# Strassen's scheme for the up products of a two-layer MLP behind linear attention: seven block products for eight, and the sums that go with it

## The chip, the cores and the metric

The kernel runs on one core of a Trainium2 chip. Times are device microseconds of one execution. Of the engines, PE multiplies matrices (PEld is its weight load), DVE works on vectors, ACT on pointwise functions and copies, POOL is GpSimd, SP issues the transfers.

## The reference

```python
def phi(x):
    proj = np.einsum('bhsd,df->bhsf', x, w_phi)
    proj = proj - np.max(np.abs(proj), axis=-1, keepdims=True)
    return np.concatenate([np.exp(proj), np.exp(-proj)], axis=-1)
...
x = attn_out.transpose(0, 2, 1, 3).reshape(2304, 512)   # linear attention, 4 x 576 tokens, 8 heads of 64
x = (sigmoid(x @ w_gate) * (x @ w_val)) @ w_out         # first layer, 512 -> 1536 -> 512
h = x @ w_in2                                           # second layer, 512 -> 2048
return np.maximum(0.01 * h, h) @ w_out2                 # 2048 -> 512
```

The weights arrive as float64 and are decoded from their bit pairs on the chip. Every product of the two layers is made of float32 operands split in two parts, hi + lo, each in the narrower fp32r type; a product is three matmuls, hi x hi, hi x lo and lo x hi (`mm3`, L50).

## The kernel before

Tokens lie on the free axis in blocks: four of 512 (one per batch) and one of 256 (the 64 last tokens of each batch, "the remainder"). The attention comes first (to about 275 us), with the first units of layer one between its pieces. Then layer one, six chunks of 256 hidden columns, and layer two, four chunks of 512 hidden columns, go through the five blocks each.

A unit is one chunk of hidden columns for one block. Its up products (`up2`, L513) run over four tiles of 128 hidden columns and four k tiles, into the PSUM banks `pg` and `pv` in turn. ACT scales the result by 0.01 (L522), DVE takes the maximum of both (L523), ACT rounds it to `gh` (L47) and DVE subtracts to give `gl` (L48). The down products (`down2`) give one 128-token piece after the other, `po`, accumulated over the chunk's tiles; DVE adds each to the sum of the chunks in SBUF (L542). The unit's down products come behind the first up tile of the next unit.

The next chunk's weights are decoded meanwhile: two masks (L77, L79), an exponent shift on ACT (L78), three DVE steps with two inputs (L80, L82, L83), a rounding on ACT (L84) and a subtraction for the low part (L86), each 128x512, for half a weight tile at a time. Steps of it are taken between the up tiles (`step`, DK).

The program's order on each engine is set by a scheduler from the order of the code. Engines hold to it.

```python
            nc.scalar.activation(out=th, in_=pg, func=ACTF.Copy, scale=0.01)
            nc.vector.tensor_tensor(out=th, in0=th, in1=pg, op=ALU.max)
            hidden(h, th, w)
```

Of the kernel before, what the change touches and what calls it, by code (L numbers as in the profile page):

```python
# [18 lines left out]
def linear_attention_moe(ctx, tc, q, k, v, w_phi, w_gate, w_val, w_out, w_in2, w_out2, out):  # L19
# [30 lines left out]
    def mm3(ps, lh, ll, rh, rl, first, last):  # L50
        nc.tensor.matmul(ps, lh, rh, start=first, stop=False)  # L51
        nc.tensor.matmul(ps, lh, rl, start=False, stop=False)  # L52
        nc.tensor.matmul(ps, ll, rh, start=False, stop=last)  # L53

    xh = [xp.tile([128, KD, w], F32R, name=f"xh{i}") for i, w in enumerate(bw)]
    xl = [xp.tile([128, KD, w], F32R, name=f"xl{i}") for i, w in enumerate(bw)]

# [1 line left out]
    CH1, CH2 = 2, 4  # L59
    NC1, NC2 = FF1 // CH1, FF2 // CH2  # L60
    NSLOT = 16
    slots = [0]
    pools = {}

    def slot():
        i = slots[0] % NSLOT
        slots[0] += 1
        pool = wpa if i < 6 else pools["wpb"]
        return pool.tile([128, 1024], F32R, tag=f"w{i}", name=f"w{i}")

    def decode(raw, hi, lo, expo):
        dp = pools["dec"]
        high, low = raw[:, :, 1], raw[:, :, 0].bitcast(U32)
        e = dp.tile([128, 512], I32, tag="e", name="e")
        m = dp.tile([128, 512], I32, tag="m", name="m")
        mf, ef = m.bitcast(F32), e.bitcast(F32)
        nc.vector.tensor_scalar(out=e, in0=high, scalar1=0x7FF00000, scalar2=0, op0=ALU.bitwise_and, op1=ALU.bitwise_or)  # L77
        nc.scalar.activation(out=e, in_=e, func=ACTF.Relu, scale=8.0, bias=ebias)  # L78
        nc.vector.tensor_scalar(out=m, in0=high, scalar1=0xFFFFF, scalar2=0x100000, op0=ALU.bitwise_and, op1=ALU.bitwise_or)  # L79
        nc.vector.scalar_tensor_tensor(out=mf, in0=low, scalar=2.0 ** -32, in1=m, op0=ALU.mult, op1=ALU.add)  # L80
        yield
        nc.vector.scalar_tensor_tensor(out=e, in0=high, scalar=-2 ** 31, in1=e, op0=ALU.bitwise_and, op1=ALU.bitwise_or)  # L82
        nc.vector.scalar_tensor_tensor(out=mf, in0=mf, scalar=2.0 ** expo, in1=ef, op0=ALU.mult, op1=ALU.mult)  # L83
        nc.scalar.copy(hi, mf)  # L84
        yield
        nc.vector.tensor_tensor(out=lo, in0=mf, in1=hi.bitcast(F32), op=ALU.subtract)  # L86
        yield

    def load_w(dst, src, r0, nr, c0, n, expo=-20):
        """Rows r0.. and columns c0.. of a weight matrix, rows on the partitions."""  # L90
        hi, lo = slot(), slot()
        dst.append([t.rearrange("p (k f) -> p k f", f=n) for t in (hi, lo)])
        kp = 512 // n
        raws = []
        for k0 in range(0, nr // 128, kp):
            raw = pools["dec"].tile([128, 512, 2], I32, tag="raw", name="raw", bufs=2)
            nc.sync.dma_start(
                out=raw.rearrange("p (k f) t -> p k (f t)", k=kp),
                in_=src[r0 + 128 * k0:r0 + 128 * (k0 + kp), 2 * c0:2 * (c0 + n)].rearrange("(k p) f -> p k f", p=128),
            )  # L100
            raws.append(raw)
        yield
        for i, raw in enumerate(raws):
            cs = slice(i * 512, i * 512 + 512)
            yield from decode(raw, hi[:, cs], lo[:, cs], expo)

    wts = {}

# [13 lines left out]
    def hidden(h, src, w):  # L122
        hi = pools["hp"].tile([128, 512], F32R, tag="gh", name="gh")[:, :w]
        lo = pools["hp"].tile([128, 512], F32R, tag="gl", name="gl")[:, :w]
        split(src, hi, lo)
        h.append((hi, lo))

    def up1(c, b, h):
        w = bw[b]
        for f in range(CH1):  # L130
            fs = slice(128 * f, 128 * f + 128)
            ps = []
            for i in range(2):
                wh, wl = wts[1, c][i]
                p = ps_m.tile([128, 512], F32, tag=("pg", "pv")[i], name=("pg", "pv")[i])[:, :w]
                ps.append(p)
                for kk in range(KD):
                    yield 0, kk
                    mm3(p, wh[:, kk, fs], wl[:, kk, fs], xh[b][:, kk], xl[b][:, kk], kk == 0, kk == KD - 1)
# [5 lines left out]
            yield 1, KD - 1  # L145

    acc = {}
    accd = {}

    def down1(c, b, h):  # L150
        (wh, wl) = wts[1, c][2]
        w = bw[b]
        for e in range(KD):
            es = slice(128 * e, 128 * e + 128)
            po = pools["po"].tile([128, 512], F32, tag="po", name="po")[:, :w]
            for f in range(CH1):
                if f:
                    yield 0
                mm3(po, wh[:, f, es], wl[:, f, es], h[f][0], h[f][1], f == 0, f == CH1 - 1)
            if c == 0 and b < B - 1:  # L160
                st = pools["tp"].tile([128, 512], F32, tag="st", name="st")
                nc.scalar.copy(st, po)
                nc.sync.dma_start(out=accd[b][:, e], in_=st)
            elif c == 0:
                nc.scalar.copy(acc[b][:, e], po)
            elif c < NC1 - 1:
                nc.vector.tensor_tensor(out=acc[b][:, e], in0=acc[b][:, e], in1=po, op=ALU.add)
            else:
# [12 lines left out]
    # Head pairs whose products with w_phi, or with the sums over k, are plain float32 ones: four passes,  # L181
    # without the work of splitting the operands, where the other engines have more to do than TensorE.
# [6 lines left out]
    # Products while the first loads are under way bring the tensor engine up to its full clock.  # L189
# [4 lines left out]
    # v of a head pair beside ones: [v_e | 1 | v_o]; the remainder's rows belong to one head each.  # L194
# [8 lines left out]
    # k_p^T [v | 1] of a pair: [kv_e | z_e | 0 | z_o | kv_o], so that 128 columns from 0 or 65 give a head.  # L203
# [38 lines left out]
    def parts(ps, n, tag, b, c):  # L242
        """The operand parts of a transposed tile: (float32,) or (hi, lo)."""
# [22 lines left out]
    def proj(x, c0, n, tag, bufs):  # L266
        """t = x @ w_phi - max|x @ w_phi| for n token tiles of a head pair."""
# [13 lines left out]
    def features(t, n, tag, bufs):  # L281
        """[exp(t), exp(-t)], tokens on the partitions."""
# [35 lines left out]
    def kv_main(p, s):  # L318
        """k_p^T [v | 1] for exp(t) or exp(-t): per head the sums of k_p v and of k_p."""
# [93 lines left out]
    pools["dec"] = p0.enter_context(tc.tile_pool(name="dec0", bufs=2))  # L413
    mid = ExitStack()
# [197 lines left out]
```

## Time and profile before

| | us |
|---|---|
| runs (3) | 1081.26, 1082.25, 1083.78; median 1082.25 |
| span of the profiled execution | 1081.0 |
| that execution's own time | one of the kernel's, not given apart; the median stands 1.25 over the span |
| PE busy | 1059.7 (98%) |
| DVE, ACT, POOL busy | 659.8 (61%), 433.9 (40%), 50.7 (5%) |
| first up product of layer two to the last down product | 680 to 1076 |

The span runs from the first to the last instruction. A matmul's duration overlaps with the next one's, so that the distance of two starts, not the duration, is what it costs; DVE's and ACT's operations overlap a little in the same way.

### The profile page before, as it was taken

The page shows a single profiled execution, that of the slowest core. Times are in us where ns is not written, and L with a number is a line of the kernel's source. Part 1 is how long each engine was busy: PE and PEld are TensorE (multiplying, and loading weights), DVE is VectorE, ACT ScalarE, POOL GpSimd, SP SyncE. Part 2 cuts the span into 40 slices and gives each one's busy share as a digit, 9 for nine tenths or more (in the row PEclk, how much of TensorE's full clock was granted, in tenths as well). Part 3 has the DMA queues.
Part 4 walks back from the last instruction along what each step waited for, and adds up shares of the span by engine and source line. Part 5 has one row for each costly group of instructions (what it writes and reads, how often), then busy time and mean ns, then how long its engine had stood idle before and what let it go on. Part 6 is the DMA issues. An engine that isn't in the chain of part 4 may idle for free.

```text
span 1081.0 us, 14504 instructions
## 1 busy us (share of the span) xinstructions
PE 1059.7 (98%) x5602; PEld 904.3 (84%) x5602; DVE 659.8 (61%) x1177; ACT 433.9 (40%) x925; POOL 50.7 (5%) x49
## 2 busy tenths in 40 slices
PE   8899999999999999999999999999999999999998
PEld 7788988889788888888888888888888888888887
DVE  5965777866489984493573774942494376333333
ACT  4665676766453431131231342533442243122121
POOL 0122121211200000000000000000000000000000
PEclk9999999999999999999999999999999999999999
DMA  6533243231363330030120210210130020000111
GB/s 156 142 79 76 64 111 75 69 87 43 93 233 115 117 97 20 1 118 1 40 78 1 75 43 1 79 39 1 39 117 2 1 78 1 1 1 20 59 39 59
DMA packets 85204, 66.69 MB, mean 62 GB/s; under 512 B 64912, under 2 KB 65040, under 8 KB 84752
## 3 DMA queue, kind: packets, MB, share of 16 engines
q1 hardware_dynamic: 85136, 65.77, 20.7%
q8 instruction: 44, 0.72, 0.3%
q14 instruction: 24, 0.20, 0.1%
HBM read 57.74 MB, written 7.94 MB: 61 GB/s over the span
## 4 chain that ended last, share of the span: by engine, by line
PE 72%; DVE 1%; issue 0%; DVEq 0%
PE po L51 10%; PE po L52 10%; PE po L53 10%; PE ph L52 6%; PE ph L51 6%; PE ph L53 6%; PE pv L51 4%; PE pv L53 4%; PE pv L52 4%; PE pg L51 4%; PE pg L52 4%; PE pg L53 4%; DVE th L143 0%; DVE e L82 0%; DVE m L80 0%
## 5 line engine op out<-in xcount | busy, mean ns | idle before, releaser
L47 ACT CAST gh<-th 128x512 fp32r<-128x512 f32 (+1 forms) x140 | 81.4, 581 | 144.3 <-DVE th L143 90.6
L48 DVE TENSOR_TENSOR gl<-th,gh 128x512 fp32r<-128x512 f32 (+1 forms) x140 | 89.1, 637 | 48.4 <-ACT gh L47 48.1
L52 PE MATMUL ph<-xl,w 128*128 128x512 f32 (+1 forms) x320 | 117.7, 368 | 0.0
L51 PE MATMUL ph<-xh,w 128*128 128x512 f32 (+1 forms) x320 | 117.7, 368 | 0.0
L53 PE MATMUL ph<-xh,w 128*128 128x512 f32 (+1 forms) x320 | 117.7, 368 | 0.0
L51 PE MATMUL po<-w,gh 128*128 128x512 f32 x288 | 112.1, 389 | 0.0
L52 PE MATMUL po<-w,gh 128*128 128x512 f32 x288 | 112.1, 389 | 0.0
L53 PE MATMUL po<-w,gl 128*128 128x512 f32 x288 | 112.0, 389 | 0.0
L522 ACT ACTIVATE th<-ph 128x512 f32<-128x512 f32 (+1 forms) x80 | 44.3, 554 | 162.8 <-PE ph L53 162.3
L523 DVE TENSOR_TENSOR th<-th,ph 128x512 f32<-128x512 f32 (+1 forms) x80 | 50.6, 632 | 75.8 <-ACT th L522 75.1
L51 PE MATMUL pv<-xh,w 128*128 128x512 f32 (+1 forms) x240 | 88.9, 370 | 1.2 <-DVE th L143 1.2
L51 PE MATMUL pg<-xh,w 128*128 128x512 f32 (+1 forms) x240 | 89.0, 371 | 0.6 <-ACT xh L47 0.6
L52 PE MATMUL pg<-xl,w 128*128 128x512 f32 (+1 forms) x240 | 89.2, 372 | 0.2 <-DVE xl L48 0.2
L53 PE MATMUL pg<-xh,w 128*128 128x512 f32 (+1 forms) x240 | 89.0, 371 | 0.0
L51 PE MATMUL po<-gh,w 128*128 128x512 f32 (+1 forms) x240 | 89.0, 371 | 0.0
L52 PE MATMUL pv<-xl,w 128*128 128x512 f32 (+1 forms) x240 | 88.8, 370 | 0.0
L53 PE MATMUL pv<-xh,w 128*128 128x512 f32 (+1 forms) x240 | 88.6, 369 | 0.0
L52 PE MATMUL po<-gl,w 128*128 128x512 f32 (+1 forms) x240 | 88.6, 369 | 0.0
L53 PE MATMUL po<-gh,w 128*128 128x512 f32 (+1 forms) x240 | 88.3, 368 | 0.0
L143 DVE SCALAR_TENSOR_TENSOR th<-th,pv 128x512 f32<-128x512 f32 (+1 forms) x60 | 37.8, 629 | 79.1 <-PE pv L53 78.4
L542 DVE TENSOR_TENSOR acc<-acc,po 128x512 f32<-128x512 f32 x54 | 37.0, 686 | 68.6 <-PE po L53 68.6
L78 ACT ACTIVATE e<-e,ebias 128x512 int32<-128x512 int32 x68 | 49.2, 724 | 54.0 <-DVE e L77 53.7
(118 smaller groups left out, 2211.5 us busy)
## 6 DMA issues: line engine op xcount, KB each, us to landing
raw<-in_moe_w_out_dram SPq DMA_DIRECT2D x28, 512.0 KB, 3.5
raw<-in_moe_w_in_dram SPq DMA_DIRECT2D x16, 512.0 KB, 3.5
raw<-in_moe_w_gate_dram SPq DMA_DIRECT2D x12, 512.0 KB, 3.9
raw<-in_moe_w_val_dram SPq DMA_DIRECT2D x12, 512.0 KB, 4.0
rb<-rd SPq DMA_DIRECT2D x32, 144.0 KB, 3.1
k<-in_k_dram SPq DMA_DIRECT2D x32, 128.0 KB, 2.9
q<-in_q_dram SPq DMA_DIRECT2D x32, 128.0 KB, 2.8
vf<-in_v_dram SPq DMA_DIRECT2D x32, 128.0 KB, 2.7
```

Of the source, the lines that this page charges most:

```text
L47: nc.scalar.copy(hi, src)
L48: nc.vector.tensor_tensor(out=lo, in0=src, in1=hi.bitcast(F32), op=ALU.subtract)
L51: nc.tensor.matmul(ps, lh, rh, start=first, stop=False)
L52: nc.tensor.matmul(ps, lh, rl, start=False, stop=False)
L53: nc.tensor.matmul(ps, ll, rh, start=False, stop=last)
L78: nc.scalar.activation(out=e, in_=e, func=ACTF.Relu, scale=8.0, bias=ebias)
L143: nc.vector.scalar_tensor_tensor(out=th, in0=th, scalar=1.0, in1=ps[1], op0=ALU.add, op1=ALU.mult)
L522: nc.scalar.activation(out=th, in_=pg, func=ACTF.Copy, scale=0.01)
L523: nc.vector.tensor_tensor(out=th, in0=th, in1=pg, op=ALU.max)
L542: nc.vector.tensor_tensor(out=a, in0=a, in1=po, op=ALU.add)
```

## The change

The up products of layer two for two blocks of 512 tokens (a pair) and 256 hidden columns are one product of 2x2 blocks (rows: two column tiles of 128; inner: two halves of k; columns: two token blocks). It is now made of seven block products for eight, in Winograd's form, by `quad`. The weights' four sums (`s`, L144 to L148) are made of each decoded tile and split in hi and lo (`sh`, `sl`). The four sums of the tokens are made once for each pair in place of the first layer's sums (`sum_steps`, `sum_parts`), split, kept in SBUF for one pair and written to DRAM (`td`); after each use in the first quad of a chunk the other pair's are loaded over them (`swap`). A quad adds the products on the way out of PSUM: five DVE additions (L734) and one copy. The remainder is multiplied as before.

Chunks of layer two are 256 columns instead of 512, eight for four, so the down products accumulate over two tiles in PSUM and the sums in SBUF are added to twice as often. The order of the units is pair, remainder, pair, and turns round with each chunk. The leaky function is one activation (L655). In layer two `gl` and `sl` are subtracted on GpSimd (`pools["lo"]`). Weights, sums of both layers and token sums share slots of 128x1024, taken and given back by hand; raw weights are fetched half a tile at a time, two ahead. Layer one is the same work, with five PSUM banks for up products (`u`) and three for down products (`p`).

```diff
-        for f in range(CH2):
-            wh, wl = wts[2, c][f // 2 * 2]
...
-            nc.scalar.activation(out=th, in_=pg, func=ACTF.Copy, scale=0.01)
-            nc.vector.tensor_tensor(out=th, in0=th, in1=pg, op=ALU.max)
-            hidden(h, th, w)
...
+        nc.scalar.copy(hi, src)
+        pools["lo"].tensor_tensor(out=lo, in0=src, in1=hi.bitcast(F32), op=ALU.subtract)
...
+                nc.vector.tensor_tensor(out=s[:, 0], in0=a21, in1=a22, op=ALU.add)
+                nc.vector.tensor_tensor(out=s[:, 2], in0=a11, in1=a21, op=ALU.subtract)
+                yield True
+                nc.vector.tensor_tensor(out=s[:, 1], in0=s[:, 0], in1=a11, op=ALU.subtract)
+                nc.vector.tensor_tensor(out=s[:, 3], in0=a12, in1=s[:, 1], op=ALU.subtract)
+                sf = s.rearrange("p s k f -> p (s k f)")
+                nc.scalar.copy(r["sh"][0], sf)
+                yield True
+                pools["lo"].tensor_tensor(out=r["sl"][0], in0=sf, in1=r["sh"][0].bitcast(F32), op=ALU.subtract)
...
+    def leaky(h, key, t):
+        w = t.shape[1]
+        tag = "" if w == 512 else "r"
+        th = tile2(w)
+        nc.scalar.activation(out=th, in_=t, func=ACTF.Lrelu)
+        hidden(h, key, th)
...
+    def sum_steps(pair):
+
+        f = {(j, i): sums[1, 2 * pair + i, j][0] for j in range(2) for i in range(2)}
+        b11, b12, b21, b22 = (f[j, i] for j in range(2) for i in range(2))
+        for o, x, y in ((b11, b12, b11), (b12, b22, b12), (b22, b22, b11), (b21, b21, b22)):
+            nc.vector.tensor_tensor(out=o, in0=x, in1=y, op=ALU.subtract)
+            yield
...
+    def swap(pair, n):
+
+        other = 1 - pair
+        if (other, n) not in td:
+            sum_parts(other, n, ts[n])
+            return
+        ts[n] = [retake(s) for s in ts[n]]
+        for k in range(2):
+            nc.sync.dma_start(out=ts[n][k][0].bitcast(F32), in_=td[other, n][:, k])
...
+        def prod(ps, a, x, first):
+            for k in range(2):
+                mm3(ps, *a[k], *x[k], first and k == 0, k == 1, skip_group_check=True)
+            ahead(1)
...
+        pa, px, py = bank("u"), bank("u"), bank("u")
+        prod(pa, W(0, 0), X(b0, 0), True)
+        s1 = tile2()
+        nc.scalar.copy(s1, pa)
+        prod(px, Sm(2), Tm(2), True)
+        then(2)
+        u2 = tile2()
+        add(u2, px, s1)
+        gap(room[0])
+        prod(py, Sm(1), Tm(1), True)
+        then(1)
+        prod(pa, W(0, 1), X(b0, 1), False)
+        yield 0, pa
+        gap(room[1])
+        prod(px, Sm(3), Tm(3), False)
+        then(3)
+        u3 = tile2()
+        add(u3, px, s1)
+        add(u3, py, u3)
+        yield 3, u3
+        gap(room[2])
+        prod(px, W(1, 1), Tm(4), False)
+        then(4)
+        add(s1, px, s1)
+        yield 2, s1
+        prod(py, Sm(4), X(b1, 1), False)
+        add(u2, py, u2)
+        yield 1, u2
+        gap(room[3])
...
+    pools["lo"] = nc.gpsimd
```

`gap(n)` puts up to n waiting down pieces there, `ahead(1)` one step of decoding.

**DVE in layer two.** Before, between the decoding (L77 to L86) stood the maximum (L523), the low part of the hidden values (L48), and elsewhere four accumulations in a row (L542):

```order
L80 SCALAR_TENSOR_TENSOR m<-raw,m 128x512
L82 SCALAR_TENSOR_TENSOR e<-raw,e 128x512
L83 SCALAR_TENSOR_TENSOR m<-m,e 128x512
L77 TENSOR_SCALAR e<-raw 128x512
L523 TENSOR_TENSOR th<-th,ph 128x512
L82 SCALAR_TENSOR_TENSOR e<-raw,e 128x512
L48 TENSOR_TENSOR gl<-th,gh 128x512
```

Now, in the first quad of a middle chunk (`q` is a quad's sum, `ps_u` and `ps_p` are banks of up and down products, L126 to L136 decode, L144 to L148 make the weights' sums):

```order
L148 TENSOR_TENSOR s<-m,s 128x256
L131 SCALAR_TENSOR_TENSOR e<-raw,e 128x512
L785 TENSOR_TENSOR acc<-acc,ps_p 128x512
L128 TENSOR_SCALAR m<-raw 128x512 x2
L785 TENSOR_TENSOR acc<-acc,ps_p 128x512
L129 SCALAR_TENSOR_TENSOR m<-raw,m 128x512
L785 TENSOR_TENSOR acc<-acc,ps_p 128x512
L132 SCALAR_TENSOR_TENSOR m<-m,e 128x512
L734 TENSOR_TENSOR q<-ps_u,q 128x512
L129 SCALAR_TENSOR_TENSOR m<-raw,m 128x512
L734 TENSOR_TENSOR q<-ps_u,q 128x512
L785 TENSOR_TENSOR acc<-acc,ps_p 128x512
```

The two L734 rows are the additions of u3; decoding and accumulations of down pieces stand ahead of them and between them.

**POOL in layer two.** Before, the last rows of POOL are those of the attention:

```order
L396 TENSOR_TENSOR rb_3534<-u0_3482,rb_3534 64x576
L396 TENSOR_TENSOR rb_3534<-u1_3499,rb_3534 64x576
```

Now it has eleven rows a chunk (the last quad's four, then the first quad of the next chunk with the weights' sums between, and the remainder's two):

```order
L169 TENSOR_TENSOR gl_7568<-q_7565,gh_7567 128x512
L169 TENSOR_TENSOR gl_7581<-q_7578,gh_7580 128x512
L169 TENSOR_TENSOR gl_7669<-q_7666,gh_7668 128x512
L152 TENSOR_TENSOR w_7763<-s_7943,w_7762 128x1024
L169 TENSOR_TENSOR gl_7725<-q_7722,gh_7724 128x512
```

The subtraction of gl has moved here from DVE, and the 1024-wide one of `sl` is new.

**PE in the first quad of a middle chunk.** The sixth product goes into the bank of the second and fifth (`ps_u_8824`), after one down piece, and the seventh into that of the third (`ps_u_8825`):

```order
L54 MATMUL ps_p_8967<-w_8419,gl_8793 128x512
L52 MATMUL ps_u_8824<-w_8569,w_8586 128x512
L53 MATMUL ps_u_8824<-w_8570,w_8586 128x512
...
L54 MATMUL ps_u_8824<-w_8569,w_8587 128x512
L52 MATMUL ps_u_8825<-xh31_92,w_8588 128x512
L53 MATMUL ps_u_8825<-xl31_93,w_8588 128x512
```

Before, the banks `pg` and `pv` took turns and nothing stood between two up tiles but down pieces.

## Rows read from the trace of the kernel before

**Rows 1.** The page: span, and busy time of each engine.

```profile
span 1081.0 us, 14504 instructions
PE 1059.7 (98%) x5602; PEld 904.3 (84%) x5602; DVE 659.8 (61%) x1177; ACT 433.9 (40%) x925; POOL 50.7 (5%) x49
```

**Rows 2.** Stretches: length, busy PE, PEld, DVE, ACT, POOL, clock, DMA share, GB/s.

```profile
296.00:311.00 15.00, 13.85 (x84) 12.24 (x83) 10.77 (x23) 7.75 (x15) 0.00 (x0) 1.00 0.81 316
...
600.00:700.00 100.00, 100.00 (x498) 85.14 (x497) 75.04 (x137) 40.98 (x72) 0.00 (x0) 1.00 0.15 48
...
680.00:1076.00 396.00, 396.00 (x1849) 331.95 (x1849) 198.84 (x341) 125.08 (x222) 0.00 (x0) 1.00 0.10 35
```

**Rows 3.** Timeline of PE: first and last of 36, and of 15, slots.

```profile
799.75 0.39 PE L51 MATMUL po<-w,gh 128*128 128x512 f32 x1
...
807.91 0.39 PE L51 MATMUL ph<-xh,w 128*128 128x512 f32 x1
...
1068.85 0.28 PE L53 MATMUL ph<-xh,w 128*128 128x256 f32 x1
...
1070.65 0.28 PE L53 MATMUL ph<-xh,w 128*128 128x256 f32 x1
```

**Rows 4.** Groups by shape on PE, layer two; L52 and L53 have the same counts.

```profile
L51 PE MATMUL po<-w,gh 128*128 128x512 f32 x288 | 112.1, 389 | 0.0
...
L51 PE MATMUL ph<-xh,w 128*128 128x512 f32 x256 | 99.7, 389 | 0.0
...
L51 PE MATMUL ph<-xh,w 128*128 128x256 f32 x64 | 18.1, 282 | 0.0
```

**Rows 5.** Groups by shape on PE, layer one: those with idle time.

```profile
L52 PE MATMUL pg<-xl,w 128*128 128x512 f32 x192 | 75.7, 394 | 0.2 <-DVE xl L48 0.2
L51 PE MATMUL pg<-xh,w 128*128 128x512 f32 x192 | 75.5, 393 | 0.6 <-ACT xh L47 0.6
...
L51 PE MATMUL pv<-xh,w 128*128 128x256 f32 x48 | 13.8, 287 | 1.2 <-DVE th L143 1.2
```

**Rows 6.** Timeline of DVE, 45 to 51 us.

```profile
44.86 0.43 DVE L77 TENSOR_SCALAR e<-raw 128x512 int32<-128x512 int32 x1 [0.35 <-DMA raw<-in_moe_w_out_dram]
45.20 0.68 DVE L278 TENSOR_TENSOR t<-ps_p,m 128x512 f32<-128x512 f32 x1
45.80 1.76 DVE L86 TENSOR_TENSOR w<-m,w 128x512 fp32r<-128x512 f32 x1
47.49 1.62 DVE L79 TENSOR_SCALAR m<-raw 128x512 int32<-128x512 int32 x1
```

**Rows 7.** Groups by shape on DVE, 680 to 1081 us.

```profile
L523 DVE TENSOR_TENSOR th<-th,ph 128x512 f32<-128x512 f32 x64 | 43.9, 686 | 72.8 <-ACT th L522 72.7
...
L86 DVE TENSOR_TENSOR w<-m,w 128x512 fp32r<-128x512 f32 x22 | 15.0, 685 | 12.3 <-ACT w L84 12.3
...
L79 DVE TENSOR_SCALAR m<-raw 128x512 int32<-128x512 int32 x20 | 8.2, 420 | 0.0
```

**Rows 8.** Groups by shape on ACT.

```profile
L522 ACT ACTIVATE th<-ph 128x512 f32<-128x512 f32 x64 | 38.2, 597 | 140.4 <-PE ph L53 140.2
...
L44 ACT ACT_TABLE_LOAD x1 | 1.3, 1283 | 0.7 <-PEq L596 0.7
```

**Rows 9.** Timelines of DVE and of POOL, 102 to 105 us.

```profile
102.94 1.50 DVE L48 TENSOR_TENSOR xlo<-ps_t,xhi 128x512 fp32r<-128x512 f32 x2 [5.56 <-ACT xhi L47]
...
101.36 2.89 POOL L396 TENSOR_TENSOR rb<-u,rb 64x576 f32<-64x576 f32 x2 [8.16 <-DMA rb<-rd]
```

**Rows 10.** Timeline of POOL, 45 to 51 us.

```profile
45.61 3.22 POOL L396 TENSOR_TENSOR rb<-u,rb 64x576 f32<-64x576 f32 x2 [42.72 <-DMA rb<-rd]
```

**Rows 11.** Timeline of the end.

```profile
1076.01 0.39 PE L53 MATMUL po<-w,gl 128*128 128x512 f32 x1
1076.44 0.69 DVE L542 TENSOR_TENSOR acc<-acc,po 128x512 f32<-128x512 f32 x1 [2.03 <-PE po L53]
```

**Rows 12.** The page's DMA issues: count, KB of one, us to landing.

```profile
raw<-in_moe_w_in_dram SPq DMA_DIRECT2D x16, 512.0 KB, 3.5
...
acc<-accd SPq DMA_DIRECT2D x3, 1024.0 KB, 7.9
```

More of the change, by code (lines that the diff above doesn't have):

```diff
@@ L1 @@
+from collections import deque
 from contextlib import ExitStack
@@ L48, in split @@
         nc.vector.tensor_tensor(out=lo, in0=src, in1=hi.bitcast(F32), op=ALU.subtract)
[L50 to L59, printed above, removed]
@@ L89, in load_w, with mm3 @@
[L89 to L96, printed above, removed]
+    def mm3(ps, lh, ll, rh, rl, first, last, **kw):
+        nc.tensor.matmul(ps, lh, rh, start=first, stop=False, **kw)
+        nc.tensor.matmul(ps, lh, rl, start=False, stop=False, **kw)
+        nc.tensor.matmul(ps, ll, rh, start=False, stop=last, **kw)
@@ L128, in up1 @@
+    accd = {}
     def up1(c, b, h):
         w = bw[b]
-        for f in range(CH1):
+        for f in range(CH):
             fs = slice(128 * f, 128 * f + 128)
@@ L452, in linear_attention_moe @@
     m_next = [10 ** 6]
-    dec = load_chunk(1, 0)
+    dec = decoded([(1, 0, i) for i in range(3)], [0])
     split(wbd, wbh, wbl)
@@ new lines, in linear_attention_moe, with bank, tile2 @@
+    turn = {"u": 0, "p": 0}
+    def bank(kind, w=512):
+        pool, tag = banks[kind][turn[kind] % len(banks[kind])]
+        turn[kind] += 1
+        return pool.tile([128, 512], F32, tag=tag, name=f"ps_{kind}")[:, :w]
+    def tile2(w=512):
+        return pools["q"].tile([128, 512], F32, tag="q", name="q")[:, :w]
+    xs = {}
+    for key in xh:
+        tag = f"{key[0]}{key[1]}" if key != B else f"{B}"
+        xs[key] = [(None, (xp, n + tag)) for n in ("xh", "xl")]
+    reserve = [0]
+    order = [(1, c, i) for c in range(1, NC1) for i in range(3)] + [(2, c, i) for c in range(NC2) for i in (0, 2)]
@@ new lines, in linear_attention_moe, with ahead, need, gap @@
+    stream = decoded(order, reserve, True)
+    def ahead(n):
+        for _ in range(n):
+            if not next(stream, None):
+                break
+    def need(*key):
+        while key not in wts:
+            if next(stream, None) is not True:
+                raise RuntimeError(f"no room for {key}: {len(free)} slots free")
+    pend = deque()
+    def gap(n):
+        for _ in range(n):
+            if pend:
+                pend.popleft()()
+    sums = {}
+    def acc(l, b, i):
+        n = 4 if l == 1 and b == B else 2
+        key = l, b, i // n
+        if key not in sums:
+            sums[key] = take(F32, "acc")
+        w = 1024 // n
+        return sums[key][0][:, w * (i % n):w * (i % n) + w]
@@ new lines, in up_pair2, with down2_piece, run @@
+    def up_pair2(c, pair, then):
+        h = {}
+        for i, t in quad(2, c, 0, pair, (3, 4, 4, 1), then):
+            leaky(h, (i // 2, 2 * pair + i % 2), t)
+        return h
+    def down2_piece(c, b, j, h):
+        def run():
+            need(2, c, 2)
+            po = bank("p")
+            js = slice(128 * j, 128 * j + 128)
+            wt = wts[2, c, 2]
+            for f in range(CH):
+                hi, lo = h[f, b]
+                mm3(po, hi[:, js], lo[:, js], wt["vhi"][:, f], wt["vlo"][:, f], f == 0, f == CH - 1)
+            a = acc(2, b, j)
```

383 lines of the change are left out of this document (244 added, 139 removed).

## The prediction

> **What bounds the kernel now.** I read the page first, then the table of stretches, the grouped rows by shape, and last the timeline. The page has PE busy for 1059.7 of 1081.0 us [rows 1]. A busy PE need not be a full one, so I looked at the second layer alone. From 680 to 1076 us PE has no idle time at all, its granted clock is 1.00, and DVE works half of the stretch [rows 2]. The slots confirm it: 36 matmuls of 512 columns start between 799.75 and 807.91 us, 0.2267 us each, and 15 of 256 columns between 1068.85 and 1070.65 us, 0.120 us each [rows 3]. The layer's 768 + 864 matmuls of 512 and 192 of 256 columns [rows 4] fill 370.0 + 23.0 = 393 of the 396 us; the last matmuls of the first layer fill the rest. So there the time is the number of matmuls, as long as the other engines keep up. In the first layer the waits of PE come to 2 us [rows 5].
>
> **What PE loses.** For one pair of 512-token blocks and 256 hidden columns the up products were 2 column tiles x 2 blocks x 4 k tiles x 3 parts = 48 matmuls; seven block products of 2 k tiles x 3 parts are 42. With 8 chunks of 256 columns and 2 pairs that is 96 matmuls fewer: 96 x 0.2267 = **-21.8 us**. A chunk of 256 columns is then 84 + 108 matmuls of 512 and 24 of 256 columns: 43.5 + 2.9 = 46.4 us of PE.
>
> **What the other engines get.** A 512-wide DVE operation starts 0.60 us after the one before it, a masking TENSOR_SCALAR 0.34 us [rows 6], and a 256-wide one I take at 0.34 too. Per chunk DVE gets 10 block additions and 18 accumulations (28 x 0.60 = 16.8 us; there were 18 per 512 columns of hidden layer, now 18 per 256), 4 half weights to decode (4 x (4 x 0.60 + 2 x 0.34) = 12.3 us, as before) and 4 sums of weight quarters (1.4 us): 30.5 of 46.4 us, where the whole layer now has 50% [rows 2]. The maximum (64 times 0.686 us [rows 7]) is gone. ACT does the leaky function at the price of the scaling it did before, 0.597 us [rows 8], gets two copies and a 1024-wide rounding a chunk, and stays under half; it loads the function's table once, 1.28 us as the first load took [rows 8], covered by the first two products (2.7 us), 1.3 us if not. The subtraction that makes gl goes to POOL, which had nothing to do in this layer [rows 2].
>
> POOL's price: two operations with two inputs of 576 columns took 2.89 us where DVE only read PSUM beside them [rows 9], 2.51 ns a column, so 1.28 us for 512, 0.64 for 256 and 2.57 for the 1024-wide low part of the sums: 8 x 1.28 + 2 x 0.64 + 2.57 = 14.1 us a chunk. POOL itself has room. Its longer step lies in the chain to the down products, 0.69 + 0.60 + 0.62 + 1.28 = 3.2 us from the end of the sixth product to gl; the order leaves 14 matmuls and the first five of the down piece there, 4.3 us, so I cost it at nothing; without that cover it is 0.6 us a quad, what POOL takes longer than DVE.
>
> **Where the gain is given back.** The two engines are in each other's way. When POOL's subtraction ran, DVE's L86 (two inputs in SBUF) took 1.76 instead of 0.685 us and L79 (a mask, SBUF only) 1.62 instead of 0.42 [rows 6, 7], and the POOL pair 3.22 instead of 2.89 [rows 9, 10]; two L48 with one input in PSUM ran through in 1.50, two times their usual 0.69 and a little [rows 9]. So a DVE operation of the first kind waits until POOL has finished, and POOL until DVE has; the additions and accumulations of the change are of the second kind, decoding is of the first. The Trainium skill says the same (SBUF — State Buffer, Who interferes with whom: the port pair is held for a whole instruction and the other blocks), and it is the rule that speaks against moving gl to POOL; the sum goes by the rows.
>
> That is walked through one first quad of a chunk, along the order, from the end of its second product. PE has 66 matmuls to the sixth product and 72 to the seventh: due at 15.0 and 16.3 us. The sixth may overwrite its bank when the first L734 addition of u3 has read it, the seventh when the second has. On DVE 30 rows stand up to there, 20 of 0.60 and 10 of 0.34: 15.4 us, and 14.2 to the end of the first addition. That would just do. But 20 of the 30 read SBUF only, and four POOL operations fall into the stretch: two gl of the quad before, the first gl of this one, and the low part of the sums (L152). I take 1.0 + 1.0 + 0.7 us for the three gl (the third meets a short row beside an accumulation) and for L152 what is left of 2.57 us after an addition of 0.60, 2.0 us; it starts beside the first addition and holds the L129 that stands between the two. First addition at 14.2 + 2.7 = 16.9 us: PE waits **1.9**. Second at 16.9 + 0.6 + 2.0 + 0.6 = 20.1 against 16.3 + 1.9 = 18.2: **1.9** more. The order has this picture in five chunks, the third to the seventh: 5 x 3.8 = **+19.0 us**. Bounds: nothing if every POOL operation meets additions (as in [rows 9]); 3 x 1.28 + 2.57 = 6.4 us of waits against the 4.7 taken, so 1.7 us more a chunk, if none does. I take the inner value, since 20 of 30 rows are of the kind that waits.
>
> **The seam.** At the start of the layer DVE gets the token sums as well: 16 operations of 1024 columns (4 differences and 4 low parts for each pair; 1.2 us each by twice 0.60), 19 us spread over the last chunk of the first layer and the first of the second, in a layer where it was busy three quarters of the time late on [rows 2]. I price this like one such chunk, **+3.8 us**; bounds 0 and 8.
>
> **The end.** Before, PE runs to 1076.0 + 0.4, one accumulation and one output transfer follow, and the span ends at 1081.0 [rows 11]. Now the last quad has no later products to cover its chain: addition 0.69, leaky 0.60, rounding 0.62, POOL 1.28, 3.2 us, under 1.36 us of product and some ready pieces: **+1.5 us**; bounds 0.5 and 3.
>
> **At nothing:** the first layer (same products; five PSUM banks for two could save the 1.2 us of [rows 5], a gain of 1 at most). The reloads of the token sums: 8 transfers of 512 KB a chunk on the SP queue, behind which the raw weights wait. Three transfers of 1 MB landed in 7.9 us by the median and the queues moved 316 GB/s in that stretch [rows 2, 12]; 4.2 MB is 13 us, and each set has some 25 us from its last use to its next. If this cover fails, the second product of the last quad waits.
>
> **Sum:** -21.8 + 19.0 + 3.8 + 1.5 = +2.5 us on a span of 1081.0, 1083.5. The span stands 1.25 us under the median of the runs shown, so I say **1085 us** (1084.8).
>
> **The rivals.**
> *DVE keeps up.* POOL's operations fall beside additions, or DVE catches up between them: 0 to 1.5 us a chunk instead of 3.8. For it: 15.4 us of DVE fit under 16.3, and the waits depend on tenths. Against it: DVE has nothing to spare there. It gives -21.8 + (0 to 7.5) + 3 + 1.5, a time of 1065 to 1073 us.
> *DVE is the bound.* Every POOL operation is met by a decoding row: 5.5 us a chunk, and 8 at the seam: -21.8 + 27.5 + 8 + 2 = +16, 1098 us. It decides from the point where the waits pass 4.7 us per first quad.
> *The reloads come late.* At the 512 KB in 3.5 us of a single transfer [rows 12] 4.2 MB take 28 us, 3 more than there are; with the raw weights in the same queue some 4 us in each of seven chunks, +28 on top of half the stalls: 1105 us.
> *POOL is quicker than scaled.* The rows have POOL at 64 partitions and 576 columns alone; if its operations here take a sixth less than scaled, 1.07 and 2.1 us, the waits shrink by 0.2 x 3 + 0.45, 1.05 a chunk, 6 us with the seam: 1079 us. Against it: the pair of [rows 9] was not held up, and 2.51 ns a column is what it took. The Trainium skill (GPSIMD Engine Reference, 2.1 Instruction dispatch) names about 2.5 cycles an element as the floor of a two-input operation, 2.1 ns at the page's 1.2 GHz, and by it the time is this rival's; the trace shows more, and the measurement decides.
>
> **Chances.** Forecast 0.47 (its own range 1079 to 1092), DVE keeps up 0.30, DVE the bound 0.13, late reloads 0.05, quicker POOL 0.05. About 0.2% (2.2 us) is what a measurement of this kernel can tell from no change. Of the forecast I put 0.06 below 1080, 0.14 within 2.2 us of 1082.25 and 0.27 above; of the quicker POOL 0.02 and 0.03. Faster is then 0.06 + 0.30 + 0.02 = 0.38, the same 0.14 + 0.03 = 0.17, slower 0.27 + 0.13 + 0.05 = 0.45. The lowest part of the first rival and the top of the second and third are the two in ten left out: 1066 to 1096.
>
> **What would show it.** Right: in the second layer the L52 rows that start the sixth and seventh product carry idle time "DVE q L734", near 3.8 us a chunk, five times; L129, L126 and L128 have means above 0.69 and 0.42 us; L785 stays at 0.686; POOL's gl lies at 1.3 to 1.7 us; the matmuls of the layer are 96 fewer. Wrong: PE without idle time between 700 and 1040 us (then the time is near 1066), idle time that ends on "DMA w<-td", or DVE rows with two SBUF inputs that keep their 0.69 us beside POOL.

## The result, and the profile after

The changed kernel takes **1098.2 us** by the median (1091.3 to 1098.8, 4 runs) against 1082.6 of the runs beside it: 1.0133 times as long, 95% interval 1.0104 to 1.0163. The forecast was 1085 us, with 1066 to 1096 as its range. The sign was right, the time 2 us beyond the range.

The page, as in [rows 1]:

```profile
span 1096.1 us, 14703 instructions
PE 1053.6 (96%) x5506; PEld 888.0 (81%) x5506; DVE 727.4 (66%) x1214; ACT 451.3 (41%) x954; POOL 168.6 (15%) x136
```

PE issues 96 matmuls fewer, yet the span is 15.1 us longer. Where the time went is read from the starts of three kinds of matmul in the two timelines:

| stage (PE) | before | after | difference | forecast |
|---|---|---|---|---|
| start to the last `ps_n` (attention) | 275.2 | 285.6 | **+10.4** | 0 |
| to the first up product of layer two | 404.9 | 404.3 | -0.6 | 0 |
| to the last down product | 395.9 | 401.9 | **+6.0** | +2.5 |
| to the end of the span | 5.0 | 4.3 | -0.7 | (in the row above) |

So the layer that was changed lost 5.3 us with the end, where the forecast had 2.5, and the attention, which the forecast did not price, lost 10.4.

**Layer two** first. PE's waits there, by what ended them (us in all, times, longest):

```profile
PE ps_u L52 <- DVE q L734: 13.1, 9, 1.7
PE ps_p L54 <- POOL gl L169: 1.8, 4, 0.7
PE ps_p L52 <- DVE acc L785: 1.5, 1, 1.5
PE ps_p L53 <- DVE gl L169: 1.0, 1, 1.0
```

The first line holds the waits that the prediction expected ahead of the sixth and seventh product of a chunk's first quad, in five chunks. Four chunks have both; the first of the five has 0.79 us ahead of the sixth and none ahead of the seventh, but the wait of 1.5 us on an accumulation, ahead of a down piece. One pair of them, in the timeline of PE:

```profile
846.64 0.39 PE L54 MATMUL ps_p<-w,gl 128*128 128x512 f32 x1
848.58 0.50 PE L52 MATMUL ps_u<-w 128*128 128x512 f32 x1 [1.55 <-DVE q L734]
848.91 0.39 PE L53 MATMUL ps_u<-w 128*128 128x512 f32 x1
...
849.84 0.40 PE L54 MATMUL ps_u<-w 128*128 128x512 f32 x1
851.78 0.50 PE L52 MATMUL ps_u<-xh,w 128*128 128x512 f32 x1 [1.55 <-DVE q L734]
```

What DVE and POOL did meanwhile, in their timelines:

```profile
847.24 0.68 DVE L132 SCALAR_TENSOR_TENSOR m<-m,e 128x512 f32<-128x512 f32 x1
847.85 0.68 DVE L734 TENSOR_TENSOR q<-ps_u,q 128x512 f32<-128x512 f32 x1
848.45 2.68 DVE L129 SCALAR_TENSOR_TENSOR m<-raw,m 128x512 f32<-128x512 uint32 x1
851.05 0.68 DVE L734 TENSOR_TENSOR q<-ps_u,q 128x512 f32<-128x512 f32 x1
```

```profile
848.19 2.39 POOL L152 TENSOR_TENSOR w<-s,w 128x1024 fp32r<-128x1024 f32 x1 [4.82 <-ACT w L150]
```

L129, a row of 0.69 us, is issued while POOL's L152 runs, and ends 0.55 us after it. The additions around it, with an input in PSUM, take 0.68 as ever. The groups of DVE by shape, 690 to 1040 us, show the same for the layer (compare L79, L86 in [rows 7]):

```profile
L785 DVE TENSOR_TENSOR acc<-acc,ps_p 128x512 f32<-128x512 f32 x103 | 69.7, 680 | 34.4 <-PE ps_p L54 34.3
L734 DVE TENSOR_TENSOR q<-ps_u,q 128x512 f32<-128x512 f32 x71 | 48.6, 685 | 48.0 <-PE ps_u L54 45.9 <-ACT q L739 1.4
L129 DVE SCALAR_TENSOR_TENSOR m<-raw,m 128x512 f32<-128x512 uint32 x26 | 26.7, 1031 | 0.1
L132 DVE SCALAR_TENSOR_TENSOR m<-m,e 128x512 f32<-128x512 f32 x26 | 22.0, 848 | 0.1
L128 DVE TENSOR_SCALAR m<-raw 128x512 int32<-128x512 int32 x26 | 21.5, 859 | 0.2
L136 DVE TENSOR_TENSOR w<-m,w 128x512 fp32r<-128x512 f32 x26 | 20.6, 793 | 2.0 <-ACT w L133 1.9
```

**The attention** lost time at two places. By the last `kv` product of each head pair, the kernel is 0.9 us late after the second pair, 6.8 after the third, 5.7 after the eighth, 8.7 after the ninth and 10.4 at the end. For the third pair, the timeline of DVE (L316 finds a projection's maximum, L318 subtracts it, the L12x and L13x rows decode):

```profile
42.67 0.69 DVE L316 TENSOR_REDUCE m<-ps_p 128x4 f32<-128x512 f32 x1 [0.60 <-PE ps_p L312]
43.28 0.68 DVE L129 SCALAR_TENSOR_TENSOR m<-raw,m 128x512 f32<-128x512 uint32 x1
...
46.48 1.89 DVE L136 TENSOR_TENSOR w<-m,w 128x512 fp32r<-128x512 f32 x1
48.29 1.88 DVE L129 SCALAR_TENSOR_TENSOR m<-raw,m 128x512 f32<-128x512 uint32 x1
50.09 0.68 DVE L318 TENSOR_TENSOR t<-ps_p,m 128x512 f32<-128x512 f32 x1
```

POOL's pair of multiplications and PE's wait, from their timelines:

```profile
46.27 3.36 POOL L436 TENSOR_TENSOR rb<-u,rb 64x576 f32<-64x576 f32 x2 [43.42 <-DMA rb<-rd]
...
50.83 0.70 PE L312 MATMUL ps_p<-wbd,xrf 128*128 128x256 f32 x2 [2.95 <-DVE t L318]
```

Seven decoding rows stand between L316 and its L318, two of them beside POOL's pair of multiplications, and PE waits 2.95 us for that L318. Before, three stood between the same two rows (then L276 and L278), and this L278 and the next one, at 45.20 [rows 6], both ran ahead of POOL's pair (45.61, [rows 10]):

```profile
40.23 0.67 DVE L276 TENSOR_REDUCE m<-ps_p 128x4 f32<-128x512 f32 x1
...
42.63 0.67 DVE L278 TENSOR_TENSOR t<-ps_p,m 128x512 f32<-128x512 f32 x1
```

The stretches (columns as in [rows 2]) show PE's clock beside the wait; first after, then before:

```profile
48.00:52.00 4.00, 1.17 (x4) 1.01 (x5) 4.00 (x6) 1.81 (x4) 1.62 (x1) 0.95 0.36 79
52.00:56.00 4.00, 4.00 (x17) 3.69 (x16) 2.17 (x5) 2.45 (x7) 0.00 (x0) 0.50 0.00 0
56.00:60.00 4.00, 4.00 (x23) 3.56 (x22) 3.00 (x6) 0.39 (x2) 0.00 (x0) 0.70 0.00 0
```

```profile
48.00:52.00 4.00, 2.35 (x15) 1.77 (x14) 3.98 (x8) 1.48 (x4) 0.83 (x1) 0.94 0.36 82
52.00:56.00 4.00, 3.52 (x14) 2.55 (x14) 3.80 (x7) 1.28 (x5) 0.00 (x0) 0.64 0.03 7
56.00:60.00 4.00, 3.98 (x26) 3.07 (x24) 1.27 (x5) 3.69 (x11) 0.00 (x0) 1.00 0.06 9
```

PE was busy 1.17 of 4 us, and in the next 4 us its granted clock was 0.50, the level of 1.2 GHz. The kernel before has a dip there too, 0.64 after 2.35 of 4 us. At the second place POOL's multiplications start later and wait for the transfer `rb`. In the timelines of POOL, ACT and PE of the kernel after, and of POOL before:

```profile
147.63 2.89 POOL L436 TENSOR_TENSOR rb<-u,rb 64x576 f32<-64x576 f32 x2 [22.08 <-DMA rb<-rd]
...
150.55 0.76 ACT L48 CAST xh<-rb 128x512 fp32r<-128x512 f32 x2 [3.54 <-POOL rb L436]
151.22 1.14 ACT L325 ACTIVATE ka<-t 128x512 f32<-128x512 f32 x2
...
152.51 0.36 PE L52 MATMUL ps_p<-wbh,xrhi 128*128 128x256 f32 x1 [3.19 <-ACT ka L325]
```

```profile
137.80 3.28 POOL L396 TENSOR_TENSOR rb<-u,rb 64x576 f32<-64x576 f32 x2 [17.93 <-ACT xhi L47]
```

ACT waits 3.54 us for POOL with the exponentials (L325) queued behind, and PE waits 3.19 us for those. It is the seventh head pair's multiplication in both; for the sixth the lag was 5.5 us (116.57 and 122.03), here it is 9.8. SP's timeline tells a part of it: `rb` is issued 10.0 us later than before (144.05 and 134.06). Its input `r` is ready on DVE 7.9 us later, and on SP a load of `v` and two of `k` now stand between the store of `r` and `rb`, 4.2 us from one to the other, where it was 3.0 with three loads of `v`. What made `r` late is open.

### The profile page after: what moved, and what is told of

It reads as the page before. It is cut to its first block, busy times and chain, and to the rows that moved or that the text cites. A ratio compares the mean times of both kernels' runs of the same rounds, so it can differ in the third digit from the quotient of the medians.

```text
span 1096.1 us, 14703 instructions
## 1 busy us (share of the span) xinstructions
PE 1053.6 (96%) x5506; PEld 888.0 (81%) x5506; DVE 727.4 (66%) x1214; ACT 451.3 (41%) x954; POOL 168.6 (15%) x136
## 4 chain that ended last, share of the span: by engine, by line
PE 56%; DVE 12%; DMA 2%; ACT 1%; issue 1%; POOL 0%; SPq 0%; ACTq 0%; POOLq 0%; DVEq 0%
PE ps_u L52 11%; PE ps_u L53 11%; PE ps_u L54 11%; PE ps_p L54 8%; PE ps_p L53 8%; PE ps_p L52 8%; DVE m L129 2%; DVE acc L785 2%; DVE q L734 1%; DVE w L136 1%; DVE m L128 1%; DVE m L132 1%; DMA raw<-in_moe_w_gate_dram 1%; DVE e L131 1%; DVE e L126 1%
## 5 line engine op out<-in xcount | busy, mean ns | idle before, releaser
L52 PE MATMUL ps_u<-xh,w 128*128 128x512 f32 (+1 forms) x592 | 214.0, 362 | 6.7 <-DVE q L734 6.3
L53 PE MATMUL ps_u<-xl,w 128*128 128x512 f32 (+1 forms) x592 | 213.6, 361 | 0.2 <-DVE xl L49 0.2
L54 PE MATMUL ps_u<-xh,w 128*128 128x512 f32 (+1 forms) x592 | 213.3, 361 | 0.0
L169 POOL TENSOR_TENSOR gl<-q,gh 128x512 fp32r<-128x512 f32 (+1 forms) x80 | 100.8, 1272 | 244.5 <-PE ps_u L54 135.0
L52 PEld LDWEIGHTS ps_u<-xh,w 128*128 128x128 f32 x592 | 111.7, 189 | 26.2 <-DVE q L734 8.0
L53 PEld LDWEIGHTS ps_u<-xl,w 128*128 128x128 f32 x592 | 111.8, 189 | 17.6 <-DVE xl L49 0.5
L54 PEld LDWEIGHTS ps_u<-xh,w 128*128 128x128 f32 x592 | 111.7, 189 | 17.2 <-DVE w L136 0.4
L785 DVE TENSOR_TENSOR acc<-acc,ps_p 128x512 f32<-128x512 f32 x126 | 85.5, 681 | 54.9 <-PE ps_p L54 54.9
L54 PE MATMUL ps_p<-w,gl 128*128 128x512 f32 x288 | 113.2, 394 | 2.0 <-POOL gl L169 1.8
L52 PE MATMUL ps_p<-w,gh 128*128 128x512 f32 x288 | 113.2, 393 | 1.7 <-DVE acc L785 1.5
L53 PE MATMUL ps_p<-w,gh 128*128 128x512 f32 x288 | 112.4, 390 | 0.0
L734 DVE TENSOR_TENSOR q<-ps_u,q 128x512 f32<-128x512 f32 x80 | 54.8, 686 | 58.1 <-PE ps_u L54 55.9
L152 POOL TENSOR_TENSOR w<-s,w 128x1024 fp32r<-128x1024 f32 x7 | 17.5, 2501 | 424.9 <-ACT w L150 424.9
L53 PE MATMUL ps_p<-gl,w 128*128 128x512 f32 (+1 forms) x216 | 79.2, 367 | 1.0 <-DVE gl L169 1.0
L52 PE MATMUL ps_p<-gh,w 128*128 128x512 f32 (+1 forms) x216 | 78.8, 366 | 0.2 <-ACT gh L168 0.2
L54 PE MATMUL ps_p<-gh,w 128*128 128x512 f32 (+1 forms) x216 | 79.0, 366 | 0.0
```

The costliest lines, as they stand in the source:

```text
L52: nc.tensor.matmul(ps, lh, rh, start=first, stop=False, **kw)
L53: nc.tensor.matmul(ps, lh, rl, start=False, stop=False, **kw)
L54: nc.tensor.matmul(ps, ll, rh, start=False, stop=last, **kw)
L169: pools["lo"].tensor_tensor(out=lo, in0=src, in1=hi.bitcast(F32), op=ALU.subtract)
L734: nc.vector.tensor_tensor(out=o, in0=x, in1=y, op=ALU.add)
L785: nc.vector.tensor_tensor(out=a, in0=a, in1=po, op=ALU.add)
```

## The experiments

Times are medians; ratios are to the runs of the kernel before in the same series (1082.8, 1083.7 and 1081.8 us).

**1 and 2: is it the decoding that the attention lost its time to?** The change rewrote the decoding of the first chunk's weights, whose steps lie between the attention's pieces. One kernel gives the change the old decoding there, the other gives the kernel before the new one. On PE, DVE, ACT and POOL the rows up to the attention's end then stand in the order of the kernel that the decoding came from.

```diff
-    dec = decoded([(1, 0, i) for i in range(3)], [0])
+    dec = decoded0([(1, 0, i) for i in range(3)])   # both loads, an empty step, then halves with an m of 512 each
```

```diff
-    dec = load_chunk(1, 0)
+    dec = load_first()   # no empty step, loads half a tile ahead, one m of 1024 for the tile
```

> The change as it is, but the first chunk's weights are decoded in the attention as they were before (a step that only issues a tile's two loads, then three steps a half); the order of all engines up to the end of the attention is then the one of before. Theory (the rewritten decoding costs the attention its 10 us): the last ps_n product starts at about 275 us as before, not 285.6, and the time falls by 9 to 11 us, to 1087 to 1089 us. Rival (the attention lost its time to something else of the change, the split token tiles or the new pools): the last ps_n stays near 285 us and the time within 3 us of 1098.

> The kernel before, with only the first chunk's decoding in the attention replaced by the change's (no step that only loads, the next half fetched when one is done, one 1024-wide buffer m in place of two of 512). Theory (this decoding costs 10 us): the last ps_n starts near 285 us and the time rises by 9 to 11 us, to 1091 to 1094 us. Rival (the rest of the change did it): no change, 1080 to 1084 us.

Measured: 1087.95 us (1.0051, 1.0033 to 1.0068) with the last `ps_n` at 275.3, and 1094.8 us (1.0098, 1.0071 to 1.0124) with it at 287.4. The second is 0.8 us over its forecast. The new decoding costs the attention 10 to 12 us with either kernel around it. The rest of the change has no part in that loss.

**3 and 4: is it POOL that the second layer lost its time to?** Both low parts go to DVE, in the change as it is and in the kernel of the first experiment.

```diff
-    pools["lo"] = nc.gpsimd
+    pools["lo"] = nc.vector
```

> The change, with both low parts of the second layer (gl and the sums' L152) on DVE instead of POOL. Theory (POOL and DVE hold each other up at SBUF): L129 and L132 are back at 0.69 us, the waits of PE on L734 fall from 13.1 us to 8 or less, though DVE now has 6.7 us more a chunk, and the time falls by 8 to 20 us, to 1078 to 1090 us. Rival (DVE is simply full in the first quad of a chunk, the lock matters little): three gl of 0.60 and a low part of 1.2 us more before the two additions, 3 us more in each of five chunks, 1105 to 1115 us.

> Both edits: the old decoding in the attention and both low parts on DVE. Theory (the two losses are separate places and add up): the gains of the two single edits add within 2 us; by the forecasts above a time of 1068 to 1080 us, under the kernel before. Rival (the waits only move, what the attention gains comes back in the layers): clearly less than the sum of the two, 1085 us or more.

Measured: 1075.9 us (0.9938, 0.9917 to 0.9959) and **1065.2 us** (0.9839, 0.9824 to 0.9854). The edit alone is worth 22.2 us, the old decoding alone 10.2, both 33.0: the two losses add up. The forecasts were right in kind and too small in size: 1075.9 lies under the 1078 to 1090 of the first, 1065.2 under the 1068 to 1080 of the second. DVE's groups in the kernel with both edits, 690 to 1040 us:

```profile
L207 DVE TENSOR_TENSOR gl<-q,gh 128x512 fp32r<-128x512 f32 x60 | 40.8, 687 | 25.3 <-ACT gh L206 25.2
...
L136 DVE TENSOR_TENSOR w<-m,w 128x512 fp32r<-128x512 f32 x26 | 17.8, 686 | 0.8 <-ACT w L133 0.3
L129 DVE SCALAR_TENSOR_TENSOR m<-raw,m 128x512 f32<-128x512 uint32 x26 | 17.3, 684 | 0.1
...
L128 DVE TENSOR_SCALAR m<-raw 128x512 int32<-128x512 int32 x26 | 10.4, 419 | 0.1
```

DVE does 6.7 us more a chunk (an estimate: eight `gl` at 0.60, two at 0.34 and a low part at 1.2 us), all decoding rows are back at the durations of [rows 7], and of PE's waits on these additions (L772 in this kernel) this is left (2.2 us with the first edit alone):

```profile
PE ps_u L52 <- DVE q L772: 2.4, 2, 2.1
```

**5, 6 and 7: which operation of POOL, and is it the result's lateness or POOL's mere work?** Against the kernel of experiment 4, L152 alone goes back to POOL, then `gl` alone. In the third nothing goes back; POOL gets a subtraction after every `gl` that nobody reads, and PE, DVE and ACT keep the order of experiment 4 row for row. In experiments 3 and 6 the scheduler also puts some 200 other rows of DVE in other places, which could be a cause by itself; the third kernel leaves that out.

```diff
+        if "spare" in pools:
+            nc.gpsimd.tensor_tensor(out=pools["spare"][:, :w], in0=hi.bitcast(F32), in1=pools["spare"][:, :w], op=ALU.subtract)
```

> e4 (old decoding in the attention, all low parts on DVE, 1065.2 us), but L152, the 1024-wide low part of the weight sums, on POOL again: one POOL operation of 2.5 us a chunk. Theory (each POOL operation that meets an SBUF-only row of DVE costs PE up to its own length in the first quad): of the seven waits of 1.9 that the prediction gave to L152 little is left, since DVE itself saves 1.2 us by it: 1064 to 1072 us. Rival (DVE has room, and only its count of rows matters): faster than e4 by the 1.2 us of DVE a chunk, 1060 to 1064 us.

> e4 with gl on POOL again (10 operations a chunk) and L152 on DVE. Theory (the lock; gl is the larger part, 8 x 1.28 + 2 x 0.64 of 14.1 us of POOL a chunk): most of the 22 us between e1 and e4 comes back, 1075 to 1086 us, with L129 well over 0.69 us. Rival (L152 alone did the harm): 1065 to 1070 us.

> e4, and after every gl of the second layer one subtraction on POOL between SBUF tiles (gh and a spare tile), whose result nobody reads. The orders of PE, DVE, ACT and SP are those of e4, and nobody waits for the spare tile. Theory (the lock: POOL and DVE keep each other off SBUF, whoever needs the result): DVE's SBUF-only rows get longer again, L129 over 0.75 us, gl over 0.8, PE waits on L734 again, and the time rises by 8 to 25 us, to 1073 to 1090 us. Rival (the change lost its time because gl came late or DVE had too many rows, and POOL's work beside it costs nothing): within 2 us of e4, 1063 to 1067 us.

Measured: 1070.0 us (0.9888, 0.9847 to 0.9929), 1079.2 us (0.9963, 0.9949 to 0.9976) and 1094.6 us (1.0103, 1.0076 to 1.0129). Against 0.9839 the first is 0.5% slower, about 5 us with runs that spread over 7, the second 1.2%, about 13 us. From the last `ps_n` to the last down product the profiled executions take 785.8 and 799.7 us, against 784.6 in experiment 4: `gl` is the larger part, and L152 alone shows only 1.2 us there, in the fastest of its four runs. The third kernel costs 29 us, 28 of them in that stretch (812.8), by work whose result nobody waits for: no wait in the layer ends on POOL. So the lateness of POOL's results is not needed for the loss. PE's waits in this kernel, and its groups on DVE and on POOL:

```profile
PE ps_p L52 <- DVE acc L825: 8.7, 6, 1.7
PE ps_p L54 <- DVE gl L207: 8.6, 9, 1.4
PE ps_u L52 <- DVE q L774: 3.9, 7, 1.6
```

```profile
L207 DVE TENSOR_TENSOR gl<-q,gh 128x512 fp32r<-128x512 f32 x57 | 69.9, 1234 | 23.9 <-ACT gh L206 23.9
L825 DVE TENSOR_TENSOR acc<-acc,ps_p 128x512 f32<-128x512 f32 x103 | 68.7, 679 | 11.5 <-PE ps_p L54 11.5
...
L129 DVE SCALAR_TENSOR_TENSOR m<-raw,m 128x512 f32<-128x512 uint32 x26 | 17.2, 681 | 0.1
```

```profile
L209 POOL TENSOR_TENSOR spare<-gh,spare 128x512 f32<-128x512 f32 x57 | 95.1, 1668 | 647.3 <-ACT gh L206 646.9
```

`gl` on DVE reads and writes SBUF alone and becomes ready with the spare subtraction, as both wait for `gh`: it takes 1.234 us by the mean instead of 0.687. The mean mixes several kinds of meeting, two of them opposite: a `gl` issued 0.5 us after POOL's row takes 1.78 us and ends 0.55 us after it, and one issued 0.11 us ahead keeps its 0.69 while POOL's row takes 1.73 instead of 1.29. The accumulations read PSUM and keep 0.679. Two signs of the forecast missed: the time lies 5 us over its range, and L129, forecast over 0.75 us, kept 0.681. So it is another row of DVE that is held here than in the change, and the 29 us price this meeting, not the change's. In experiment 6, too, L129 was held little (0.725 us), and the mask L128 more (0.844 for 0.42).

**8: what is the scheme itself worth?** The kernel of experiment 4 with `up_plain` for every block in layer two: eight products, no sums, no reloads.

```diff
-                h = up_pair2(c, u, (lambda k, u=u: swap(u, k)) if n == 0 else (lambda k: None))
+                h = {}
+                for b in (2 * u, 2 * u + 1):
+                    h.update(up_plain(2, c, b, 2))
```

> e4 with the second layer's up products done as eight block products, without any sums of weights or tokens: 96 matmuls of 512 columns more (21.8 us at 0.2267), no stores and reloads of token sums, 10 block additions and four quarter sums a chunk less on DVE. Theory (the scheme is worth its matmuls, less the few us that PE still waits in e4, 5.9 us by its slots): 1065.2 + 21.8 - 4 to 6, 1081 to 1083 us, the time of the kernel before. Rival (the gain of e4 comes in part from the smaller chunks, the single activation or the five banks, not from the scheme): 1070 to 1078 us.

Measured: 1081.4 us (0.9984, 0.9966 to 1.0001), and PE has no idle time in layer two. The scheme is worth 1.45% or 15.7 us between these kernels: its 21.8 us of matmuls less the 5.8 us by which slots are too long in experiment 4. The traces have the same: 395.8 and 380.4 us from the layer's first up product to its last down product. Chunk size, banks and activation together bring nothing that stands clear of the noise.

**9 and 10: what in the decoding?** The old decoding has an empty step ahead of each tile, two `m` of 512 columns, and both loads of a tile issued at that step. The first two come back alone, each on the kernel of experiment 3; the loads were not tried by themselves.

```diff
             m = dp.tile([128, 1024], I32, tag="m", name="m", bufs=1)
+            if not sums:
+                yield True
```

```diff
-                mi = m[:, cs]
+                mi = m[:, cs] if sums else dp.tile([128, 512], I32, tag="m", name="m")
```

> e3 (the change with low parts on DVE, 1075.9 us), and the change's decoding in the attention gets back one thing alone: a first step for each tile that decodes nothing, so that the decoding stands one step later in the attention's order. The shared 1024-wide m stays. With both this step and two 512-wide m the order would be that of e4 (1065.2). Theory (the decoding comes too early and pushes the projections' L316 and L318 behind it on DVE): the last ps_n starts at 275 to 279 us instead of 283 to 287, the time is 1065 to 1070 us. Rival (the single buffer m does it, a half's decoding waits for the last half's): as e3, 1074 to 1078 us.

> e3, and the change's decoding in the attention gets back the other thing alone: two 512-wide buffers m that alternate, in place of one of 1024. No empty step. Theory (the missing step does the harm): as e3, 1074 to 1078 us, the last ps_n at 283 us or later. Rival (the single m does it): 1065 to 1070 us, the last ps_n at 275 to 279 us.

Measured: 1075.5 us (0.9937, 0.9918 to 0.9955), the last `ps_n` at 285.4; and 1070.0 us (0.9897, 0.9878 to 0.9916), with 275.9 in the profiled execution, which was the fastest of its four (1064.9; the others 1069 to 1072). The empty step alone gives back nothing, against what I expected; the second `m` alone some 5 of the 10.7 us, and in one execution of four all of them. Only the old decoding as a whole (experiment 4) gave 1064 to 1066 us every time.

Both traces have that first subtraction of the third pair (L318 in the change) ahead of POOL's pair, at 44.57 with the step and at 44.29 with two `m`, so that row's place is not the whole loss. With the step alone the wait moves on: at 58.28 us a decoding row waits 2.22 us for ACT's rounding, a subtraction of the maximum stands behind it, and PE waits 2.08 us for that one; the kernel is 2.8 us late after the third pair and 7.2 after the fourth. The kernel with two `m` has nearly the change's order up to the attention's end (17 rows of DVE, 27 of PE and 9 of ACT stand elsewhere). Why it differs so much between executions is open.

**11: the leaky function alone**, in the kernel before.

```diff
-            nc.scalar.activation(out=th, in_=pg, func=ACTF.Copy, scale=0.01)
-            nc.vector.tensor_tensor(out=th, in0=th, in1=pg, op=ALU.max)
+            nc.scalar.activation(out=th, in_=pg, func=ACTF.Lrelu)
```

> The kernel before with the leaky function by one activation, and nothing else: the maximum on DVE goes (72 operations, 64 of 512 columns), PE's products stay. Theory (PE has no idle time in that layer, so an operation less on DVE is worth nothing): within 2 us of the kernel before, 1080.5 to 1084.5 us. Rival (the shorter chain to gh and gl, 0.6 us less, saves a wait, or the other activation function costs table loads): 3 us or more off to either side.

Measured: 1083.4 us (1.0008, 0.9997 to 1.0019). No difference: PE has no idle time in that layer, with the maximum or without it.

**12: the last waits.** The kernel of experiment 4 with the down pieces moved.

```diff
-        for i, t in quad(2, c, 0, pair, (3, 4, 4, 1), then):
+        for i, t in quad(2, c, 0, pair, (2, 3, 3, 1), then):
```

> e4 with the eight ready down pieces of a quad spread 2, 3, 3 in place of 3, 4, 1, so that two more pieces (2.7 us) stand ahead of the sixth product, where PE still waits for the first L734 addition in e4 (2.3 us in one chunk). Theory (PE waits there for DVE, and more cover takes the wait away): 1062 to 1065 us, no slot over 1 us ahead of a ps_u product. Rival (the wait moves to the third product, which now has less cover): 1065 to 1070 us.

Measured: **1062.3 us** (0.9824, 0.9803 to 0.9844), the best of all, though its interval overlaps that of experiment 4. No slot ahead of a sixth product is too long any more; one wait of 0.8 us on an addition is left, ahead of another product early in the layer, so the rival had a little of it. From the last `ps_n` to the last down product it takes 781.2 us, 3.4 less than experiment 4.

## Why the prediction was wrong, and where it was right

**The step that failed is "At nothing".** It names the first layer and the reloads, and has no word on the attention, though the diff rewrites the decoding that runs inside it: a step for each tile dropped, two buffers `m` made one. I had priced the decoding by its rows ("as before") and not by what stands beside them. Experiments 1 and 2 put that term at +10 to +12 us, the traces at +10.4, of the 12.6 us between the forecast span (1083.5) and the measured one (1096.1). The other 2.2 are 2.8 more in the second layer than the sum had, and 0.6 less in the first. The lock that the prediction describes acts there too: its [rows 6] and [rows 10] come from just the place where the third pair now waits. Which part of the decoding costs how much stays open in part (experiments 9 and 10).

**The rival "DVE is the bound"** names the measured time, 1098 us, by chance. It has the whole +16 us in the second layer, with 5.5 us of waits in each first quad; the layer and the end lost 5.3, with 3.6 in a quad, and the rest of the 15 us lies in the attention. In the rival of late reloads the terms named give 1101 to 1103 us, not 1105; the forecast does not hang on it.

**The matmuls, -21.8:** right. The 15.7 us of experiment 8 and the 5.8 us by which slots are too long in experiment 4 make 21.5.

**The quads, +19.0:** right in cause and size, and in place but for one wait. By PE's slots beyond 0.227 us the five first quads lost 2.9 us once and about 3.6 four times, 17.4 in all. In the quad shown, the second product ends at 831.4; the walk had the first addition done 16.9 us and the second 20.1 us later, and they were done after 17.1 and 20.3.

**The seam, +3.8:** 2.8 measured. **The end, +1.5:** 2.0 up to the last down product, and 0.7 back behind it. POOL's longer step, costed at nothing, made PE wait 1.8 us in four places, in the first chunks and the last. What no step had is a rest of 4.5 us, nearly all in pieces of 0.1 and 0.2: PE's slots after a wait, and the first two at the second product of each chunk, take 0.34 instead of 0.227. All slots too long in layer two make 26.7 us, where the steps had 24.3.

**POOL's price:** the `gl` that nothing held up took 1.29 us (1.28 forecast), L152 2.37 to 2.45 (2.57), and a `gl` of 256 columns 0.73 (0.64). The three lie on a line, an estimate from these rows: 0.19 us for an operation and 2.15 ns a column. The forecast scaled 576 columns without the fixed part, which does little at 512. "POOL is quicker than scaled", by a sixth, is refuted for `gl`, and L152 was 5 to 8% quicker.

**"DVE has nothing to spare there"**, said against the rival "DVE keeps up", was true only with POOL beside it: with 6.7 us more of its own a chunk, and no POOL, DVE keeps up in nearly every chunk (experiment 4). A full DVE and a held DVE look alike in busy time: 13 us of waits at 66% busy after, 2.4 us at 69% in experiment 4.

**"The reloads come late"** fell: `w<-td` landed in 4.9 us by the median, 56 times, and no wait of PE ends on it. **The leaky function at nothing:** right (experiment 11); the table was loaded once, in 1.283 us, like the first load [rows 8].

The Trainium skill says (SBUF — State Buffer, Who interferes with whom) that of DVE and GpSimd the one that issues first has the port pair they share for its whole instruction, and the other is blocked. The trace agrees: L129, issued 0.26 us into an L152 of 2.39 us, took 2.68 us, and the additions from PSUM beside it kept 0.68. That the low parts belong on DVE here is what experiments 3 and 4 measured.

## What to carry to other kernels

Moving work to an idle engine is no gift if the two hold each other up, as POOL does with DVE's rows on SBUF alone: count the held rows of the busy engine, not the idle engine's free time; here two moves that "freed" DVE of 6.7 us a chunk cost 22 us. When a diff rewrites a helper, price it at every place that calls it, also in the stage that the change is not about: the rewritten decoding in the attention cost half of what the new scheme saves. And an algorithm's saving should be measured by itself: with both losses undone, the seven products make the kernel 1.6% faster than before (1.8% with the pieces moved).

## What the runs showed of the hardware that I had not expected

- Work on POOL that nobody needs can cost as much as work that somebody waits for: 29 us for one subtraction beside each `gl` on DVE, where `gl` and L152 on POOL cost 22. POOL's operation grew as well, to 1.668 us from 1.29.
- A wait of PE costs a little more than itself: after the 1.55 us above, the first matmul's successor starts 0.33 us later (848.58, 848.91), not 0.227.
- Behind the attention's wait the granted clock was lower too: after a stretch with PE busy for 1.17 of 4.00 us, 0.50 and 0.70 were granted in the next two stretches (0.64 and 1.00 before the change, after 2.35 of 4.00), while beside the two waits of 1.55 us shown in layer two it was 1.00, the level of 2.4 GHz.
